# Unsplit float32 projections on quarters of the array, and sums of squares on ScalarE, in a fused attention and gated-MLP kernel

## The chip, the core and the metric

The kernel runs on one core of a Trainium2 chip as one launch. The time is device microseconds (us) of that core, the median of three runs. A core has a matrix engine (TensorE, PE in the profile; PEld is its weight load), a vector engine (VectorE, DVE), an engine for activation functions (ScalarE, ACT), a general one (GpSimd, POOL), and queues that issue DMA transfers (SyncE, SP, issues nearly all of them here). Each engine works through its own instructions in order and waits on semaphores for the others. On-chip data lies in SBUF; matrix products land in PSUM, eight banks of 128 partitions by 512 float32 values.

## The reference, cut to what matters

```python
batch, n_heads, seq, head_dim = 8, 8, 576, 64          # q, k, v; float32
def phi(x):                                            # x scaled by 64 ** -0.25
    proj = x @ omega.T                                 # 64 -> 128 features
    sq = sum(x * x, axis=-1) / 2
    h = proj - sq
    return exp(h - max(h, axis=-1)) / sqrt(128)
q_p, k_p = phi(q_s), phi(k_s)
kv, z = k_p^T @ v, sum(k_p, axis=seq)                  # per batch and head
attn = (q_p @ kv) / (q_p @ z + 1e-6)                   # [4608 tokens, 512]
gate, val = sigmoid(attn @ w_gate), attn @ w_val       # 512 -> 1536
out = (gate * val) @ w_out                             # 1536 -> 512
```

## The kernel before

The program has two stages. The **first stage** holds the attention and, as filler, the early third of the gated products (four of the twelve column tiles of the hidden layer). The **second stage** holds the other eight column tiles (line 558, `gw`) and the output product (line 671, `po`), both with a seven-product scheme for 2 by 2 blocks; the change does not touch their arithmetic, but their banks come from `any_bank`, which it does touch.

**Attention.** Batches are taken in four pairs `u`, heads in four pairs `p`. For one `(u, p)` the two batches have 1152 tokens, nine tiles of 128. A tile of k or q arrives with the 64 dimensions of two heads on the 128 partitions (`raw`, line numbers in `source`). `projected` makes the projection of a group of at most two tiles: ScalarE writes the rounded high part `hi` (L764), GpSimd the rest `lo` (L767), and TensorE does three products of 128 by 128 weights with 256 columns for each tile (L775 to L777), against `omH` and `omL`, which hold omega for both heads in a block-diagonal 128 by 256 matrix, in the type float32r. One bank of PSUM takes two tiles. VectorE takes the row maximum (`mx`, L787), and from it and the sums of squares `sq` the bias terms: `hm` (L793), then for k `nb` (L832), for q `sub` (L898) and the whole exponent `h` (L900). For k, ScalarE does the exponential with a bias for each tile and head, 128 columns at a time (L842), and `pkv` (L867) multiplies with v. For q, TensorE transposes `h` into `pt` (L914), ScalarE takes the exponential into `qp` (L919), `pn` (L931) multiplies with kv, VectorE divides (`den`, `inv`, `x`, L942 to L948), TensorE transposes back into `px` (L956), ScalarE copies it (L965) and SyncE stores it. The float32 products `pkv` and `pn` already use half the columns of the array at a time (64 columns of weights).

**Sums of squares.** `norms` loads q and k a second time with tokens on the partitions (`nat`), a tile of 128 by 512 at a time. ScalarE squares it (L726), VectorE sums each head's 64 columns (L730) and, when the four or five tiles of a batch are there, scales the sums (L747).

**Filler products.** `products` multiplies the finished attention (`xe`, split into two parts by ScalarE at L408 and GpSimd at L418) with the early column tiles: `gv`, L445. Weights that come as float64 words are made into float32 on VectorE and GpSimd (lines 155 to 169, 332) in between. Until the first `xe` is there, each projection is followed by four products into a bank that is never read (`unread`, L781).

**The order.** The order of each engine's work in the first stage is written out by a planner, the class `Turns`: it plays the kernel through with a cost for each instruction (`act`, `dve`, `pool_`, `PE_LAG` and so on) and fixes for each engine which step is next. Steps ask for places (`shelf`): eight banks, of which projections may hold four (`pps`) and filler products two (`gvs`); buffers in SBUF have places of their own. Attention goes by rank, filler products have the lowest rank. The second stage's operands lie in memory that the first stage's buffers held.

Of the kernel before, what the change touches and what calls it, by code (L numbers as in the profile page):

```python
# [9 lines left out]
F32 = mybir.dt.float32  # L10
# [18 lines left out]
GROUPS = {"k": (((0, 1), (2, 3), (4,)), ((5, 6), (7, 8))), "q": (((0, 1), (2, 3)), ((4,), (5, 6), (7, 8)))}  # L29
# [16 lines left out]
UNREAD = 4  # L46

RAWS, SPLITS, KPS, VS, HS, XS, NATS = 6, 5, 8, 3, 4, 3, 2
KVS, PPS, GVS = 13, 4, 2
CVS = 2  # L50
# [122 lines left out]
def attn_glu_kernel(ctx: ExitStack, tc, qT, kT, qn, kn, va, om, ident, w, out):  # L173
# [12 lines left out]
    om_sb = const.tile([P, 2 * M], F32, name="om_sb")  # L186
# [3 lines left out]
    omH = const.tile([P, 2 * M], F32R, name="omH")  # L190
    omL = const.tile([P, 2 * M], F32R, name="omL")
    split(nc, omH, omL, om_sb)
# [3 lines left out]
    def bank(i, name):  # L196
        return ps.tile([P, 512], F32, tag=f"bank{i}", bufs=1, name=name)

    def any_bank(name):

        n_banks[0] += 1
        return bank(n_banks[0] % 8, name)
# [51 lines left out]
    def act(n, pointer=False):  # L254
        return (165 if pointer else 120) + 0.833 * n

    def dve(n):
        return (n + 140) / 0.96

    def dve2(n):  # L260
        return (n / 2 + 140) / 0.96
# [4 lines left out]
    PE_LAG, LAG, ISSUE, LANDS = 260, 100, 420, 3200  # L266


    banks, pps, gvs = shelf(8), shelf(PPS), shelf(GVS)
# [153 lines left out]
    def products():  # L423
        yield from after(x_ready[0][0], 0)
        unread.clear()
        banks.put(spare, turns.now)
# [30 lines left out]
    spare = banks.take()  # L457
    unread = [bank(spare, "unread")]
# [234 lines left out]
    def span(name, b):  # L693
# [5 lines left out]
        "raw": shelf(RAWS), "split": shelf(SPLITS), "kp": shelf(KPS), "v": shelf(VS), "h": shelf(HS), "qp": shelf(HS),  # L699
        "kv": shelf(KVS), "kmid": shelf(NP), "x": shelf(XS), "xs": shelf(2), "nat": shelf(NATS), "x2": shelf(2),  # L700
# [4 lines left out]
    for u in range(U):  # L705
        for b in range(2):
            for n in ("k", "q"):
                sq_ready[n, u, b] = Event(turns)
# [8 lines left out]
    def norms(pool, name, u, b, src):  # L717

        t0, t1 = span(name, b)
        s = pool.tile([P, MID + 1, H], F32, tag="ss", bufs=2, name=f"ss{name}{u}_{b}")[:, : t1 - t0]  # L720
        every = Event(turns, t1 - t0)

        def squares(t, x, i, at):
            at, (k,) = yield from turn("ACT", at, places["x2"])
            x2 = spot(pool, "x2", k, [P, DM], f"x2{name}{u}_{t}")
            nc.scalar.activation(out=x2, in_=x, func=AF.Square)  # L726
            at = use("ACT", at, act(DM), LAG)
            places["nat"].put(i, at)
            at = yield "DVE", at, None
            nc.vector.tensor_reduce(  # L730
                out=s[:, t - t0, :], in_=x2.rearrange("p (h d) -> p h d", d=D), axis=AX.X, op=ALU.add
            )
            at = use("DVE", at, dve(DM), LAG)
            places["x2"].put(k, at)
            every.set(at)

        rank = order["n" + name, u, b]
# [6 lines left out]
        at = yield from after(every, 0)  # L744
        at = yield "DVE", at, None
        sq = pool.tile([P, MID + 1, H], F32, tag="sq", bufs=4 * U, name=f"sq{name}{u}_{b}")
# [3 lines left out]
        at = use("DVE", at, 190, LAG)  # L750
        sqs[name, u, b] = sq
        sq_ready[name, u, b].set(at)

    def projected(pool, name, u, p, b, raw, t0, tiles, at, last):
# [3 lines left out]
        at, (i,) = yield from turn("ACT", at, places["split"])  # L758
        hi, lo = (
            spot(pool, tag, i, [P, 2 * P], f"{tag}{id_}", F32R)[:, : nt * P] for tag in ("hi", "lo")  # L760
        )
        o = (tiles[0] - t0) * P
        x = raw[:, o : o + nt * P]
        nc.scalar.activation(out=hi, in_=x, func=AF.Copy)  # L764
        at = use("ACT", at, act(nt * P), LAG)
        at = yield "POOL", at, None
        nc.gpsimd.tensor_tensor(out=lo, in0=x, in1=hi.bitcast(F32), op=ALU.subtract)  # L767
        at = use("POOL", at, pool_(nt * P), LAG)
        last.set(at)
        at, (place, own) = yield from turn("PE", at, banks, pps)  # L770
        pp = bank(place, f"pp{id_}")[:, : nt * 2 * M]
        for k, t in enumerate(tiles):
            c = slice(k * P, (k + 1) * P)
            o = pp[:, k * 2 * M : (k + 1) * 2 * M]
            nc.tensor.matmul(o, lhsT=lo[:, c], rhs=omH, start=True, stop=False)  # L775
            nc.tensor.matmul(o, lhsT=hi[:, c], rhs=omL, start=False, stop=False)  # L776
            nc.tensor.matmul(o, lhsT=hi[:, c], rhs=omH, start=False, stop=True)  # L777
        at = use("PE", at, 3 * nt * 118, PE_LAG)
        for o in unread:
            for _ in range(UNREAD):  # L780
                nc.tensor.matmul(o[:, : 2 * M], lhsT=hi[:, :P], rhs=omH, start=True, stop=True)  # L781
            use("PE", at - PE_LAG, UNREAD * 118, 0)
        places["split"].put(i, at)
        pp = pp.rearrange("p (i m) -> p i m", m=M)
        at = yield "DVE", at, None
        mx = pool.tile([P, 4], F32, tag="mx", bufs=12, name=f"mx{id_}")[:, : 2 * nt]
        nc.vector.tensor_reduce(out=mx, in_=pp, axis=AX.X, op=ALU.max)  # L787
        at = use("DVE", at, dve(nt * 2 * M), LAG)
        at = yield from after(sq_ready[name, u, b], at)
        at = yield "DVE", at, None  # L790
        s = sqs[name, u, b][:, tiles[0] - t0 : tiles[-1] + 1 - t0, 2 * p : 2 * p + 2]
        hm = pool.tile([P, 2, 2], F32, tag="hm", bufs=12, name=f"hm{id_}")[:, :nt]
        nc.vector.scalar_tensor_tensor(  # L793
            out=hm, in0=mx.rearrange("p (t h) -> p t h", h=2), scalar=SCALE, in1=s,
            op0=ALU.mult, op1=ALU.subtract,
        )
        at = use("DVE", at, 160, LAG)
        return at, id_, pp, hm, s, place, own
# [15 lines left out]
    def keys(pool, u, p, b):  # L814
# [12 lines left out]
        def group(tiles):  # L827
            at_, id_, pp, hm, s, place, own = yield from projected(pool, "k", u, p, b, raw, t0, tiles, at, last)
            nt = len(tiles)
            at_ = yield "DVE", at_, None  # L830
            nb = pool.tile([P, 2, 2], F32, tag="nb", bufs=12, name=f"nb{id_}")[:, :nt]
# [3 lines left out]
            at_ = use("DVE", at_, 160, LAG)  # L835
# [3 lines left out]
            for i, t in enumerate(tiles):  # L839
                kp[t] = x[:, 2 * i : 2 * i + 2, :]  # L840
                for h in range(2):
                    nc.scalar.activation(  # L842
                        out=kp[t][:, h, :], in_=pp[:, 2 * i + h, :], func=AF.Exp,
                        bias=nb[:, i, h : h + 1], scale=SCALE,
                    )
            at_ = use("ACT", at_, 2 * nt * act(M, True), LAG)
# [4 lines left out]
            banks.put(place, at_)  # L851
            pps.put(own, at_)
# [31 lines left out]
    def queries(pool, u, p, b):  # L884
# [6 lines left out]
        def group(tiles):  # L891
            at_ = yield from after(kexp_ready[u, p, b], start)
            at_, id_, pp, hm, s, place, own = yield from projected(pool, "q", u, p, b, raw, t0, tiles, at_, last)
            nt = len(tiles)
            n = 2 * nt
            at_, (hi,) = yield from turn("DVE", at_, places["h"])
            sub = pool.tile([P, 2, 2], F32, tag="sub", bufs=12, name=f"sub{id_}")[:, :nt]
            nc.vector.tensor_tensor(out=sub, in0=s, in1=hm, op=ALU.add)  # L898
            h_sb = spot(pool, "h", hi, [P, 4, M], f"h{id_}")[:, :n]
            nc.vector.scalar_tensor_tensor(  # L900
                out=h_sb,
                in0=pp,
                scalar=SCALE,
                in1=sub.rearrange("p t h -> p (t h)").unsqueeze(2).broadcast_to([P, n, M]),
                op0=ALU.mult,
                op1=ALU.subtract,
            )
            at_ = use("DVE", at_, 240 + dve(n * M), LAG)
            banks.put(place, at_)
            pps.put(own, at_)  # L910
            at_, (place, qi) = yield from turn("PE", at_, banks, places["qp"])
            pt = bank(place, f"pt{id_}")[:, : n * P].rearrange("p (i s) -> p i s", s=P)
            for i in range(n):
                nc.tensor.transpose(out=pt[:, i, :], in_=h_sb[:, i, :], identity=id_sb)  # L914
            at_ = use("PE", at_, n * 109, PE_LAG)
            places["h"].put(hi, at_)
# [34 lines left out]
            at_ = use("DVE", at_, 440 + dve(n * D), LAG)  # L951
# [35 lines left out]
    attended = [U * NP * sum(len(g) for g in GROUPS["q"])]  # L987
# [148 lines left out]
```

## Time and profile before

| | |
|---|---|
| median of 3 runs | 1238.59 us (1237.07 to 1239.68) |
| the profiled execution's own time | 1236.42 us |
| its span, first to last instruction | 1234.6 us |
| mean granted clock of TensorE | 0.966 |
| PE busy | 1138.8 us, 92% |
| DVE busy | 888.4 us, 72% |
| ACT busy | 529.6 us, 43% |
| POOL busy | 572.8 us, 46% |
| second stage's first product (L558) starts at | 581.2 us |

The shares are means over both stages. Busy time of an engine is the time in which at least one of its instructions was in work; matmuls overlap, so the rate of a run of matmuls is read from their starts, not from the mean duration of one. In a row of a group, what stands after the bar is the busy time of the group, the mean duration of one instruction in ns, and the engine's idle time before them with what ended it.

### The profile page before, as it was taken

The page shows a single profiled execution, that of the slowest core. Times are in us where ns is not written, and L with a number is a line of the kernel's source. Part 1 is how long each engine was busy: PE and PEld are TensorE (multiplying, and loading weights), DVE is VectorE, ACT ScalarE, POOL GpSimd, SP SyncE. Part 2 cuts the span into 40 slices and gives each one's busy share as a digit, 9 for nine tenths or more (in the row PEclk, how much of TensorE's full clock was granted, in tenths as well). Part 3 has the DMA queues.
Part 4 walks back from the last instruction along what each step waited for, and adds up shares of the span by engine and source line. Part 5 has one row for each costly group of instructions (what it writes and reads, how often), then busy time and mean ns, then how long its engine had stood idle before and what let it go on. Part 6 is the DMA issues. An engine that isn't in the chain of part 4 may idle for free.

```text
span 1234.6 us, 26447 instructions
## 1 busy us (share of the span) xinstructions
PE 1138.8 (92%) x10092; PEld 1062.0 (86%) x10092; DVE 888.4 (72%) x1885; ACT 529.6 (43%) x1168; POOL 572.8 (46%) x591
## 2 busy tenths in 40 slices
PE   4869989999898998779999999999998899999998
PEld 4758978887787777557999999999998899999998
DVE  5888798898888998623665665666569577777775
ACT  4646676474545554342422323223225243433331
POOL 2647273455635644434566666666657311111111
PEclk7889999999999989888999999999999899999999
DMA  6646477386756755364233233323347675665653
GB/s 234 235 152 220 151 237 242 101 279 234 233 192 217 242 172 171 107 238 140 121 124 123 91 125 124 125 96 124 148 139 252 190 228 184 192 191 188 188 189 112
DMA packets 107744, 217.75 MB, mean 176 GB/s; under 512 B 10848, under 2 KB 48992, under 8 KB 105312
## 3 DMA queue, kind: packets, MB, share of 16 engines
q1 hardware_dynamic: 102288, 206.54, 49.5%
q10 hardware_dynamic: 5328, 9.51, 2.0%
q8 instruction: 80, 1.31, 0.4%
q14 instruction: 48, 0.39, 0.1%
HBM read 141.82 MB, written 74.19 MB: 175 GB/s over the span
## 4 chain that ended last, share of the span: by engine, by line
PE 70%; DVE 11%; issue 6%; POOL 5%; DMA 5%; ACT 2%; SPq 1%; POOLq 0%; DVEq 0%; ACTq 0%
PE gw L558 26%; PE po L671 20%; PE gv L445 8%; PE pnq L931 3%; PE ptq L914 3%; PE pkv L867 2%; DVE mxk L787 1%; PE ppq L775 1%; PE pxq L956 1%; PE ppk L775 1%; DVE hmq L793 1%; DMA ye<-ye 1%; POOL xe L418 1%; PE ppk L777 1%; PE ppk L776 1%
## 5 line engine op out<-in xcount | busy, mean ns | idle before, releaser
L558 PE MATMUL gw<-xl,u 128*128 128x256 f32 x3024 | 363.9, 283 | 6.0 <-DVE u L538 3.8
L558 PEld LDWEIGHTS gw<-xl,u 128*128 128x128 f32 x3024 | 362.2, 190 | 7.6 <-DVE u L538 5.0
L671 PE MATMUL po<-u,yh 128*128 128x256 f32 x1512 | 273.1, 283 | 0.0
L671 PEld LDWEIGHTS po<-u,yh 128*128 128x128 f32 x1512 | 235.1, 191 | 0.0
L671 PE MATMUL po<-u,yl 128*128 128x256 f32 x756 | 214.4, 284 | 5.0 <-POOL yl L147 3.5
L445 PE MATMUL gv<-xe,wh 128*128 128x512 f32 (+1 forms) x640 | 198.0, 386 | 11.4 <-POOL xe L418 11.4
L146 ACT ACTIVATE yh<-yr 128x896 fp32r<-128x896 f32 x108 | 98.9, 948 | 166.8 <-DVE yr L662 58.5
L671 PEld LDWEIGHTS po<-u,yl 128*128 128x128 f32 x756 | 144.7, 191 | 5.6 <-POOL yl L147 3.7
L445 PEld LDWEIGHTS gv<-xe,wh 128*128 128x128 f32 x640 | 116.2, 193 | 32.3 <-POOL xe L418 15.3
L147 POOL TENSOR_TENSOR yl<-yr,yh 128x896 fp32r<-128x896 f32 x18 | 39.3, 2183 | 218.9 <-ACT yh L146 165.9
L445 PE MATMUL gv<-xe,wl 128*128 128x512 f32 (+1 forms) x320 | 123.8, 387 | 12.0 <-ACT xe L408 11.9
L662 DVE TENSOR_TENSOR yr<-yr 128x128 f32<-128x128 f32 x144 | 68.0, 505 | 62.1 <-DMA yr<-ye 61.5
L147 DVE TENSOR_TENSOR yl<-yr,yh 128x896 fp32r<-128x896 f32 x90 | 96.1, 1099 | 12.9 <-ACT yh L146 12.7
L538 DVE TENSOR_TENSOR u<-gw,p 128x256 f32<-128x256 f32 x144 | 60.7, 421 | 60.2 <-PE gw L558 52.1
L767 POOL TENSOR_TENSOR loq<-rawq,hiq 128x256 fp32r<-128x256 f32 (+1 forms) x80 | 60.3, 768 | 83.1 <-ACT hiq L764 57.3
L767 POOL TENSOR_TENSOR lok<-rawk,hik 128x256 fp32r<-128x256 f32 (+1 forms) x80 | 61.5, 777 | 69.4 <-ACT hik L764 64.9
L842 ACT ACTIVATE kpk<-ppk,nbk 128x128 f32<-128x128 f32 x256 | 71.9, 393 | 34.1 <-DVE nbk L832 33.9
L445 PEld LDWEIGHTS gv<-xe,wl 128*128 128x128 f32 x320 | 62.1, 194 | 22.3 <-ACT xe L408 13.1
L591 POOL TENSOR_TENSOR yl<-yl,gl 128x256 f32<-128x256 f32 x36 | 36.0, 1000 | 81.1 <-issue 39.1
L588 ACT ACTIVATE gl<-gl 128x768 f32<-128x768 f32 x36 | 30.5, 846 | 90.0 <-DVE gl L538 90.0
L914 PE MATMUL ptq<-id_sb,hq 128*128 128x128 f32 x288 | 47.4, 284 | 21.9 <-DVE hq L900 19.9
L919 ACT ACTIVATE qpq<-ptq 128x512 f32<-128x512 f32 (+1 forms) x80 | 44.5, 557 | 46.8 <-PE ptq L914 46.1
(218 smaller groups left out, 2209.7 us busy)
## 6 DMA issues: line engine op xcount, KB each, us to landing
yl<-yl SPq DMA_DIRECT2D x36, 896.0 KB, 4.0
yr<-yl SPq DMA_DIRECT2D x72, 448.0 KB, 4.2
xr<-xT SPq DMA_DIRECT2D x68, 256.0 KB, 4.5
u<-w SPq DMA_DIRECT2D x14, 896.0 KB, 6.8
v<-va SPq DMA_DIRECT2D x32, 330.0 KB, 4.4
natk<-kn SPq DMA_DIRECT2D x36, 256.0 KB, 3.5
natq<-qn SPq DMA_DIRECT2D x36, 256.0 KB, 3.2
out<-o ACTq DMA_DIRECT2D x36, 256.0 KB, 2.9
```

Of the source, the lines that this page charges most:

```text
L146: nc.scalar.activation(out=hi, in_=x, func=AF.Copy)
L147: (lo_engine or nc.vector).tensor_tensor(out=lo, in0=x, in1=hi.bitcast(F32), op=ALU.subtract)
L445: nc.tensor.matmul(gv, lhsT=u[:, s], rhs=v, start=(m == 0), stop=(m == 3 * KC - 1))
L538: return nc.vector.tensor_tensor(out=o, in0=a, in1=b, op=ALU.add)
L558: nc.tensor.matmul(o, lhsT=u[:, k, s], rhs=v[:, kc, :], start=(first and m == 0), stop=(m == 5), skip_group_check=not first,)
L662: nc.vector.tensor_tensor(out=raw[:, o], in0=raw[:, a], in1=raw[:, b], op=op)
L671: nc.tensor.matmul(o, lhsT=u[:, i, :], rhs=v[:, k, :], start=(j + m == 0 and n in (1, 6, 5, 4)), stop=(j == NPAIR - 1 and m == 2), skip_gr ...
L767: nc.gpsimd.tensor_tensor(out=lo, in0=x, in1=hi.bitcast(F32), op=ALU.subtract)
L842: nc.scalar.activation(out=kp[t][:, h, :], in_=pp[:, 2 * i + h, :], func=AF.Exp, bias=nb[:, i, h : h + 1], scale=SCALE,)
L914: nc.tensor.transpose(out=pt[:, i, :], in_=h_sb[:, i, :], identity=id_sb)
L919: nc.scalar.activation(out=qp, in_=pt, func=AF.Exp)
L931: nc.tensor.matmul(pn[r, 2 * i + h, :], lhsT=qp[:, 2 * i + h, r], rhs=kvs[u, p, bb][:, h, :], start=True, stop=True,)
```

## The change

Four things are done together.

- **Projection.** The split is gone (`hi`, `lo`, `omH`, `omL`). A tile is projected by four float32 matmuls, one for each quarter of the array: 64 rows (one head's dimensions) by 64 columns (half of the tile's tokens) as weights, and 128 columns of omega moving. The two heads, which use different rows, write to different banks.
- **Groups.** A group has up to four tiles in a place of two banks. There are two such places (`pairs`) and four single banks for all else (`pt`, `pn`, `px`, `pkv`, `gv`). The small steps on VectorE are done once for a group of four. After the projection, q goes on two tiles at a time (`attended_tiles`). `any_bank` of the second stage hands out the four single banks and the four halves of the pairs in turn.
- **Sums of squares.** ScalarE squares each head's 64 columns in place with the scale in the activation and writes the sum by its accumulator: eight instructions for a tile, given out four at a time. VectorE's reduction and scaling are gone.
- **The rest.** The products that nobody reads are gone. The planner's costs and the numbers of buffers are other ones.

```diff
-GROUPS = {"k": (((0, 1), (2, 3), (4,)), ((5, 6), (7, 8))), "q": (((0, 1), (2, 3)), ((4,), (5, 6), (7, 8)))}
+GROUPS = {"k": (((0, 1, 2, 3), (4,)), ((5, 6, 7, 8),)), "q": (((0, 1, 2, 3),), ((4,), (5, 6, 7, 8)))}
-UNREAD = 4
-RAWS, SPLITS, KPS, VS, HS, XS, NATS = 6, 5, 8, 3, 4, 3, 2
-KVS, PPS, GVS = 13, 4, 2
+RAWS, KPS, VS, HS, QPS, XS, NATS = 6, 4, 3, 3, 4, 3, 4
+KVS, GVS, CVS = 15, 2, 2
+BANKS, PAIRS = 4, 2
+    def two_banks(i, name):
+        return ps.tile([P, 2, 512], F32, tag=f"pair{i}", bufs=1, name=name)
     def any_bank(name):
+        i = n_banks[0] % (BANKS + 2 * PAIRS)
         n_banks[0] += 1
-        return bank(n_banks[0] % 8, name)
+        if i < BANKS:
+            return bank(i, name)
+        if not halves:
+            two = two_banks((i - BANKS) // 2, name)
+            halves.extend((two[:, 0], two[:, 1]))
+        return halves.pop(0)
     def act(n, pointer=False):
-        return (165 if pointer else 120) + 0.833 * n
+        return (140 if pointer else 85) + 0.833 * n
     def dve(n):
-        return (n + 140) / 0.96
+        return (n + 65) / 0.96
-    PE_LAG, LAG, ISSUE, LANDS = 260, 100, 420, 3200
+    PE_LAG, LAG, ISSUE, LANDS = 210, 140, 420, 3500
-    banks, pps, gvs = shelf(8), shelf(PPS), shelf(GVS)
+    banks, pairs, gvs = shelf(BANKS), shelf(PAIRS), shelf(GVS)
         def squares(t, x, i, at):
-            nc.scalar.activation(out=x2, in_=x, func=AF.Square)
+            for half in range(2):
+                at = yield "ACT", at, None
+                for h in range(half * H // 2, (half + 1) * H // 2):
+                    part = x[:, h * D : (h + 1) * D]
+                    nc.scalar.activation(
+                        out=part, in_=part, func=AF.Square, scale=SCALE * 0.5**0.5,
+                        accum_out=sq[:, t - t0, h : h + 1],
+                    )
+                at = use("ACT", at, H // 2 * act(D), LAG)
-            nc.vector.tensor_reduce(
-                out=s[:, t - t0, :], in_=x2.rearrange("p (h d) -> p h d", d=D), axis=AX.X, op=ALU.add
-            )
-        nc.vector.tensor_scalar(
-            out=sq[:, : t1 - t0], in0=s, scalar1=SCALE * SCALE / 2.0, scalar2=None, op0=ALU.mult
-        )
     def projected(pool, name, u, p, b, raw, t0, tiles, at, last):
-        nc.scalar.activation(out=hi, in_=x, func=AF.Copy)
-        nc.gpsimd.tensor_tensor(out=lo, in0=x, in1=hi.bitcast(F32), op=ALU.subtract)
-        at, (place, own) = yield from turn("PE", at, banks, pps)
-            nc.tensor.matmul(o, lhsT=lo[:, c], rhs=omH, start=True, stop=False)
-            nc.tensor.matmul(o, lhsT=hi[:, c], rhs=omL, start=False, stop=False)
-            nc.tensor.matmul(o, lhsT=hi[:, c], rhs=omH, start=False, stop=True)
-        at = use("PE", at, 3 * nt * 118, PE_LAG)
-        for o in unread:
-            for _ in range(UNREAD):
-                nc.tensor.matmul(o[:, : 2 * M], lhsT=hi[:, :P], rhs=omH, start=True, stop=True)
+        at, (place,) = yield from turn("PE", at, pairs)
+        pp = two_banks(place, f"pp{id_}").rearrange("p h (t m) -> p h t m", m=M)[:, :, :nt]
+        for k, t in enumerate(tiles):
+            o = (t - t0) * P
+            for one in range(2):
+                for h in range(2):
+                    r = HALVES[one ^ h]
+                    nc.tensor.matmul(
+                        pp[r, h, k, :], lhsT=raw[HALVES[h], o + r.start : o + r.stop], rhs=om_sb[HALVES[h], :],
+                        start=True, stop=True,
+                    )
+        at = use("PE", at, nt * 220 + 100, PE_LAG)
...
+                if i and i % 2 == 0:
+                    at_ = yield "ACT", use("ACT", at_, 4 * act(M, True), 0), None
                 for h in range(2):
                     nc.scalar.activation(
-                        out=kp[t][:, h, :], in_=pp[:, 2 * i + h, :], func=AF.Exp,
+                        out=kp[t][:, h, :], in_=pp[:, h, i, :], func=AF.Exp,
...
+            h_sb = spot(pool, "h", hi, [P, 2, 4, M], f"h{id_}")[:, :, :nt]
+            pairs.put(place, at_)
+            used = Event(turns, (nt + 1) // 2)
+            turns.start(released(used, "h", hi), rank)
+            for i in range(0, nt, 2):
+                turns.start(attended_tiles(h_sb[:, :, i : min(i + 2, nt)], tiles[i : i + 2], at_, used), rank)
+        def attended_tiles(h_sb, tiles, at_, used):
...
-    om = np.zeros((P, 2 * M), omega.dtype)
-    om[:D, :M] = omega.T
-    om[D:, M:] = omega.T
+    om = np.concatenate([omega.T, omega.T], axis=0)
```

More of the change, by code (lines that the diff above doesn't have):

```diff
@@ L423, in products @@
     def products():
-        yield from after(x_ready[0][0], 0)
-        unread.clear()
-        banks.put(spare, turns.now)
         for c, (o, n) in enumerate(chunks):
@@ L707, in attn_glu_kernel @@
             for n in ("k", "q"):
-                sq_ready[n, u, b] = Event(turns)
+                for t in range(*span(n, b)):
+                    sq_ready[n, u, t] = Event(turns)
             for p in range(NP):
@@ L719, in norms @@
         t0, t1 = span(name, b)
-        s = pool.tile([P, MID + 1, H], F32, tag="ss", bufs=2, name=f"ss{name}{u}_{b}")[:, : t1 - t0]
-        every = Event(turns, t1 - t0)
+        sq = pool.tile([P, MID + 1, H], F32, tag="sq", bufs=4 * U, name=f"sq{name}{u}_{b}")
+        sqs[name, u, b] = sq
+        rank = order["n" + name, u, b]
         def squares(t, x, i, at):
[L724 to L727, printed above, removed]
-            places["nat"].put(i, at)
-            at = yield "DVE", at, None
-            nc.vector.tensor_reduce(
-                out=s[:, t - t0, :], in_=x2.rearrange("p (h d) -> p h d", d=D), axis=AX.X, op=ALU.add
-            )
[L733 to L737, printed above, removed]
+            for half in range(2):
[7 more added lines that the diff above has]
+                at = use("ACT", at, H // 2 * act(D), LAG)
+            places["nat"].put(i, at)
+            sq_ready[name, u, t].set(at)
         for t in range(t0, t1):
@@ L757, in projected @@
         nt = len(tiles)
[L758 to L766, printed above, removed]
-        nc.gpsimd.tensor_tensor(out=lo, in0=x, in1=hi.bitcast(F32), op=ALU.subtract)
@@ L787, in projected @@
         nc.vector.tensor_reduce(out=mx, in_=pp, axis=AX.X, op=ALU.max)
         at = use("DVE", at, dve(nt * 2 * M), LAG)
-        at = yield from after(sq_ready[name, u, b], at)
+        for t in tiles:
+            at = yield from after(sq_ready[name, u, t], at)
         at = yield "DVE", at, None
[L791 to L796, printed above, removed]
@@ L797, in projected @@
-        at = use("DVE", at, 160, LAG)
-        return at, id_, pp, hm, s, place, own
+        s = sqs[name, u, b][:, tiles[0] - t0 : tiles[-1] + 1 - t0, 2 * p : 2 * p + 2].rearrange("p t h -> p h t")
+        hm = pool.tile([P, 2, 4], F32, tag="hm", bufs=12, name=f"hm{id_}")[:, :, :nt]
+        nc.vector.scalar_tensor_tensor(out=hm, in0=mx, scalar=SCALE, in1=s, op0=ALU.mult, op1=ALU.subtract)
+        at = use("DVE", at, 100, LAG)
+        return at, id_, pp, hm, s, place
     def source(pool, name, u, p, b, src):
@@ L827, in group @@
         def group(tiles):
-            at_, id_, pp, hm, s, place, own = yield from projected(pool, "k", u, p, b, raw, t0, tiles, at, last)
+            at_, id_, pp, hm, s, place = yield from projected(pool, "k", u, p, b, raw, t0, tiles, at, last)
             nt = len(tiles)
             at_ = yield "DVE", at_, None
-            nb = pool.tile([P, 2, 2], F32, tag="nb", bufs=12, name=f"nb{id_}")[:, :nt]
+            nb = pool.tile([P, 2, 4], F32, tag="nb", bufs=12, name=f"nb{id_}")[:, :, :nt]
             nc.vector.scalar_tensor_tensor(
@@ L834, in group @@
             )
[L835 removed]
+            at_ = use("DVE", at_, 100, LAG)
             tag = "kmid" if tiles[0] == MID else "kp"
@@ L892, in group @@
             at_ = yield from after(kexp_ready[u, p, b], start)
-            at_, id_, pp, hm, s, place, own = yield from projected(pool, "q", u, p, b, raw, t0, tiles, at_, last)
+            at_, id_, pp, hm, s, place = yield from projected(pool, "q", u, p, b, raw, t0, tiles, at_, last)
+            nt = len(tiles)
+            at_, (hi,) = yield from turn("DVE", at_, places["h"])
+            sub = pool.tile([P, 2, 4], F32, tag="sub", bufs=12, name=f"sub{id_}")[:, :, :nt]
+            nc.vector.tensor_tensor(out=sub, in0=s, in1=hm, op=ALU.add)
@@ L894, in group @@
+        def attended_tiles(h_sb, tiles, at_, used):
+            id_ = f"q{u}_{p}_{tiles[0]}"
             nt = len(tiles)
             n = 2 * nt
[L896 to L907, printed above, removed]
@@ L908, in group @@
-            at_ = use("DVE", at_, 240 + dve(n * M), LAG)
-            banks.put(place, at_)
-            pps.put(own, at_)
             at_, (place, qi) = yield from turn("PE", at_, banks, places["qp"])
             pt = bank(place, f"pt{id_}")[:, : n * P].rearrange("p (i s) -> p i s", s=P)
-            for i in range(n):
-                nc.tensor.transpose(out=pt[:, i, :], in_=h_sb[:, i, :], identity=id_sb)
+            for i in range(nt):
+                for h in range(2):
+                    nc.tensor.transpose(out=pt[:, 2 * i + h, :], in_=h_sb[:, h, i, :], identity=id_sb)
@@ L915, in group @@
             at_ = use("PE", at_, n * 109, PE_LAG)
-            places["h"].put(hi, at_)
+            used.set(at_)
             at_ = yield "ACT", at_, None
@@ L986, in attn_glu_kernel @@
                     order[n, u, p, b] = float(len(order))
-    attended = [U * NP * sum(len(g) for g in GROUPS["q"])]
+    attended = [U * NP * sum((len(tiles) + 1) // 2 for g in GROUPS["q"] for tiles in g)]
     keep = ctx.enter_context(tc.tile_pool(name="keep", bufs=1))
```

45 lines of the change are left out of this document (15 added, 30 removed).

## The prediction

> **What bounds the kernel now.** I read the page's busy shares first, then the busy time by stage, because the change touches the first stage only (a row of the windows: the stretch, its length, the busy time of PE, PEld, DVE, ACT and POOL with their instructions, the granted clock, and the DMA's share and GB/s).
>
> ```profile
> span 1234.6 us, 26447 instructions
> PE 1138.8 (92%) x10092; PEld 1062.0 (86%) x10092; DVE 888.4 (72%) x1885; ACT 529.6 (43%) x1168; POOL 572.8 (46%) x591
> ...
> 0.00:124.00 124.00, 87.21 (x960) 79.94 (x962) 97.17 (x213) 68.05 (x190) 64.97 (x68) 0.86 0.62 211
> 124.00:494.00 370.00, 346.37 (x3498) 293.27 (x3495) 325.73 (x772) 211.78 (x587) 187.65 (x200) 0.98 0.61 206
> 494.00:591.00 97.00, 75.26 (x412) 60.76 (x410) 38.39 (x72) 33.09 (x54) 36.25 (x26) 0.88 0.49 173
> 591.00:1234.60 643.60, 629.95 (x5232) 627.99 (x5232) 427.09 (x831) 216.68 (x339) 283.93 (x297) 0.99 0.45 153
> ```
>
> The last window is the second stage: PE is busy 630 of 643.6 us with work that the change leaves alone. What can move is when it starts, and PE's trace has that start, 653 us before the end:
>
> ```profile
> 581.21 7.73 PE L558 MATMUL gw<-xl,u 128*128 128x256 f32 x60
> ```
>
> In the middle window PE is at 346 of 370 us (94%) and DVE at 326 (88%): two engines near full, since the filler products take whatever PE has left. In the early window DVE leads, 97 of 124 us, and PE is idle 37 us. After 494 us attention ends and PE is idle 21.7 us of 97. The chain of waits shows why there:
>
> ```profile
> 482.54 18.11 issue
> 500.69 2.44 POOL c L169
> ...
> 558.10 23.29 PE gv L445 x89
> ```
>
> The late weights (`c`) wait on POOL behind steps of DVE, and the last 89 filler products come at the end of the same chain. So stage one is set by PE's amount of work plus 82 us of PE idle time (37, 24 and 22), 37 of it where DVE is the fuller engine.
>
> **The projections on PE.** The trace of PE, start and duration of each step:
>
> ```profile
> 478.91 0.28 PE L777 MATMUL ppq<-omH,hiq 128*128 128x256 f32 x1
> 479.03 0.28 PE L775 MATMUL ppq<-omH,loq 128*128 128x256 f32 x1
> 479.14 0.28 PE L776 MATMUL ppq<-omL,hiq 128*128 128x256 f32 x1
> 479.26 0.28 PE L777 MATMUL ppq<-omH,hiq 128*128 128x256 f32 x1
> 479.38 0.60 PE L914 MATMUL ptq<-id_sb,hq 128*128 128x128 f32 x4
> 479.91 0.69 PE L931 MATMUL pnq<-kv,qpq 128*64 128x66 f32 x16
> ...
> 479.91 0.55 PEld L931 LDWEIGHTS pnq<-kv,qpq 128*64 128x64 f32 x16 [0.17 <-issue]
> ...
> 481.14 0.69 PE L931 MATMUL pnq<-kv,qpq 128*64 128x66 f32 x16
> 481.76 0.50 PE L445 MATMUL gv<-xe,wl 128*128 128x512 f32 x1
> 482.09 0.63 PE L445 MATMUL gv<-xe,wh 128*128 128x512 f32 x2
> ```
>
> Starts of the split projection lie 0.117 us apart (478.91 to 479.26 in three steps). There are 288 tiles of three, so it takes 864 x 0.117 = 101 us, and at a lower clock early on somewhat more.
>
> The new form is 288 x 4 float32 matmuls. The code has eight matmuls in a full group of `pnq`, the trace 16 records: a float32 matmul is two. So a tile is eight records of 128 columns. Four float32 transposes of 128 columns take 0.53 us (479.38 to 479.91, the change of form included), at most 0.13 for a record; 256 float32r columns took 0.117. I take 0.117 for one record alone, 0.94 us for eight in a row. What overlaps? `pnq` has records of 66 columns on halves of the array's columns. By the same rate a record is 0.06 us and 16 are 0.97; they took 0.62 (481.14 to 481.76): column halves do overlap. No row of this trace shows row halves. From below: all four quarters together, 0.94 / 4 = 0.234 a tile, while eight weight loads at `pnq`'s rate (0.55 / 16) are 0.275. From above: only column halves together, 0.47. I take 0.25, next to the load rate, since the loads are the row that exists: 288 x 0.25 = 72 us. Going in and out of a quartered form costs too. `pnq`'s loads wait 0.17 us for nothing that shows, and the first `gv` after it holds PE for 0.33 us where 0.23 is normal (481.76 to 482.09; 512 columns are two times 0.117). I take 0.2 us for each of the 96 new groups: 19 us, and half of it as the lower end. PE then does 91 us in place of 101, **10 us less**. The ends are 67 + 10 = 77 (24 less) and 135 + 19 = 154 (53 more).
>
> **The products nobody reads.**
>
> ```profile
> L781 PE MATMUL unread<-omH,hik 128*128 128x256 f32 x72 | 13.9, 324 | 0.0
> L781 PE MATMUL unread<-omH,hiq 128*128 128x256 f32 x40 | 6.3, 279 | 0.0
> ```
>
> 112 products, 20 us busy, all in the early window, where PE has 37 us idle. They delay what is behind them in PE's queue (chiefly transposes and `pkv`), but leave no bound; I fold them into the early term. What they may do for the clock: it was 0.86 in that window with PE busy 70% of it, and 0.88 in the window after 494 with 78%. PE would be busy 67 of 124 us.
>
> **What leaves the other engines.**
>
> Groups of VectorE:
>
> ```profile
> L832 DVE SCALAR_TENSOR_TENSOR nbk<-sqk,hmk 128x4 f32<-128x4 f32 (+1 forms) x80 | 30.8, 405 | 0.0
> ...
> L793 DVE SCALAR_TENSOR_TENSOR hmk<-mxk,sqk 128x4 f32<-128x4 f32 (+1 forms) x80 | 24.0, 319 | 0.0
> L730 DVE TENSOR_REDUCE ssq<-x2q 128x8 f32<-128x512 f32 x36 | 23.8, 674 | 1.7 <-ACT x2q L726 1.6
> L730 DVE TENSOR_REDUCE ssk<-x2k 128x8 f32<-128x512 f32 x36 | 23.8, 677 | 8.0 <-ACT x2k L726 8.0
> L793 DVE SCALAR_TENSOR_TENSOR hmq<-mxq,sqq 128x4 f32<-128x4 f32 (+1 forms) x80 | 22.7, 313 | 0.0
> L898 DVE TENSOR_TENSOR subq<-sqq,hmq 128x4 f32<-128x4 f32 (+1 forms) x80 | 21.6, 270 | 0.0
> ```
>
> DVE loses 47.6 us of reductions. The four kinds of small steps go from 80 runs to 48 each: 99 us x 0.4 = 40 less, if a run with eight columns costs what one with four did (they hardly depend on width). The maxima and `h` keep their columns and lose fixed parts, which I leave at zero. That is 88 us of 461 in stage one (97 + 326 + 38). POOL loses the 160 subtractions behind `hi`; it was not full, but two queues leave the way from `raw` to PE.
>
> Groups of ScalarE, and a run of its exponentials from the trace in order of time:
>
> ```profile
> L764 ACT ACTIVATE hik<-rawk 128x256 fp32r<-128x256 f32 (+1 forms) x80 | 30.4, 408 | 23.8 <-PE ppq L777 10.0 <-PE unread L781 6.9 <-DMA rawk<-kT 1.8
> L764 ACT ACTIVATE hiq<-rawq 128x256 fp32r<-128x256 f32 (+1 forms) x80 | 30.3, 414 | 16.5 <-PE ppk L777 6.1 <-PE ppq L777 5.8 <-PE unread L781 2.0
> ...
> L726 ACT ACTIVATE x2q<-natq 128x512 f32<-128x512 f32 x36 | 22.9, 661 | 9.2 <-DMA natq<-qn 6.3 <-DVE ssq L730 2.4 <-ACT x2q L726 0.5
> L726 ACT ACTIVATE x2k<-natk 128x512 f32<-128x512 f32 x36 | 22.7, 634 | 8.6 <-DMA natk<-kn 8.5
> ```
> ```profile
> 469.76 2.18 ACT L842 ACTIVATE kpk<-ppk,nbk 128x128 f32<-128x128 f32 x8 [2.30 <-DVE nbk L832]
> ```
>
> ACT loses 106 us (`hi` and the squares) and gets 576 squares of 64 columns. Eight exponentials of 128 columns with a bias take 2.18 us, about 0.26 each in a row, so 0.15 is the lower end for half as wide ones without a bias. No row shows the accumulator's write; from above I take a second instruction as long as one of these, 0.51 in all. I choose 0.25, nearer to the plain one: 144 us. ACT goes from 313 us in stage one to 351, with ends of 293 and 501.
>
> **The sum.** Of the 288 products at L775, one for each tile, the early window has 67:
>
> ```profile
> 0.00:124.00 124.00, 23.03 (x67) 14.47 (x67) 0.86 0.62 211
> ```
>
> From the profiled execution, 1236.4 us (span 1234.6 and 1.8 around it; the median of the runs is 2.2 above it):
> - PE's projections: -10.
> - Early window: DVE loses about a quarter of its 88 us here (67 of 288 tiles), 22 us of 97. PE waits there for chains that also go through ACT and DMA, so I take half: -11 (0 to -22).
> - Middle window: of PE's 24 us idle half comes back with DVE at some 70%: -12 (0 to -20).
> - After 494: the order will be another one with other planner costs, and the idle 22 us can grow or shrink: 0, plus or minus 10.
>
> Together -33: 1203.4, and **1206 us** as a median of runs. The second stage's PE time is taken as it is: its banks still come round after eight, a pair after both its halves are free.
>
> **The rivals.**
> - *The row halves take turns* (slower). 0.47 us a tile makes the projections 53 us dearer; early and middle idle time takes 11 and 12 of it: 1236.4 + 30 + 2.2 = 1269. It decides from (101 + 23 - 19) / 288 = 0.365 us a tile. For it: the trace has no two row halves at work. Against: `pnq`'s column halves overlap.
> - *ACT becomes the bound.* At 0.51 a square the middle window has 212 + 0.75 x (294 - 106) = 353 of 370 us: fuller than DVE was. Nothing is regained, chains get longer: about 1243. It decides where ACT passes DVE's 326 us, at 0.45 a square.
> - *The quarters overlap in part.* `pnq`'s 0.97 us of records took 0.55 in its loads, 1.76 times on two halves; squared for quarters that is 3.1 of 4, or 0.94 / 3.1 = 0.30 us a tile. The projections then take 87 + 19 us, 5 more than today instead of 10 less: 1221. It is a shade of the row halves' case, and `pnq` is the only row on it. TensorE: Matmul & The Clock Gate in the Trainium skill, Part 3 (Packing small matmuls), gives 3.07 times for four packed tiles of 32 rows, near the same; no run so far shows row tiles here.
> - *The early stage gains nothing, because the array's clock falls.* Without the unread products PE has 67 us of work there at a clock of 0.86. At half speed this is 67 x 0.86 / 0.5 = 115 us of 124, and the -11 is gone: 1217. Against it: 0.86 was granted with 37 us idle. TensorE: Matmul & The Clock Gate in the Trainium skill, Part 1 (The HAM clock gate), says that an idle window of about 3.4 us is enough for half the pulses; the trace's mean neither shows nor excludes such windows.
> - *PSUM places run short.* A group of four k tiles holds a pair for 1.1 us of PE, then some 2 on DVE and 2 on ACT; a q group about 4 in all, so 64 groups and 32 single tiles hold two pairs for some 180 us each out of 490 if nothing queues. If queues double that and PE idles 25 us more in the middle: 1236.4 - 10 - 11 + 25 + 2.2 = 1243. Against: no releaser in the chain is a bank today.
> - *The gain is hidden by the end.* If the chain of late weights after 482 us only moves with the planner's order, the -11 stands and the rest goes: about 1227.
> - *PE fills up.* 0.234 a tile, short changes of form, and nearly all reachable idle time back: -24 - 20 - 20: about 1175.
>
> **How the numbers follow.** Forecast (1188 to 1223) 0.48; quarters in part 0.08; clock 0.05; gain hidden 0.08; PE fills up 0.09; ACT 0.08; places 0.07; row halves 0.07. The first five are faster, less 0.03 at their edges; 0.2% is 2.5 us, about what a measurement of this kernel can tell from no change. Faster 0.75, same 0.05 (those edges and a little of the two at 1243), slower 0.20. A range of 1176 to 1250 leaves out the row halves, the worst of the two at 1243 (0.04 together) and half of "PE fills up".
>
> **What would show it.** Right: `ppk` and `ppq` as 2304 records in the count, about 1.0 to 1.1 us from the first of a full group to the last; DVE in the middle below 75%; ACT there at 60 to 70%; PE idle under 15 us in the middle; `gw` starting near 548 instead of 581 us. Wrong: a group of 1.9 us (row halves in turn); squares spaced by 0.45 us or more; PE waiting at projections for `kpk` or `hq` of two groups before (places); an end still led by late weights with PE idle over 30 us; or a second stage that is no longer 653 us from the first `gw` on.

## The result, and the profile after

The changed kernel takes **1301.75 us** (median of four runs, 1300.0 to 1303.25) against 1238.2 before: 1.0512 times as long, 95% interval 1.0493 to 1.0531. The forecast was 1206, and the range ended at 1250. It is slower by 63.5 us.

The page of the changed kernel and the busy time of its stages, in the columns of the prediction's windows:

```profile
span 1301.0 us, 29349 instructions
PE 1125.4 (86%) x11420; PEld 1014.4 (78%) x11420; DVE 799.6 (61%) x1572; ACT 566.8 (44%) x2087; POOL 452.2 (35%) x431
...
0.00:124.00 124.00, 68.09 (x1098) 57.42 (x1099) 81.28 (x138) 106.53 (x691) 32.37 (x28) 0.85 0.68 228
124.00:494.00 370.00, 340.31 (x4811) 272.22 (x4810) 278.14 (x582) 225.81 (x1030) 117.91 (x94) 0.99 0.65 222
494.00:591.00 97.00, 85.92 (x490) 74.92 (x489) 35.91 (x60) 28.69 (x47) 34.68 (x31) 0.96 0.31 110
591.00:1301.00 710.00, 631.04 (x5028) 609.88 (x5026) 404.23 (x794) 205.82 (x320) 267.30 (x280) 0.99 0.41 136
```

PE, DVE and POOL have less to do, ACT has 37 us more and is far from full over the whole span, and the time is longer: waiting has come in somewhere. The second stage's first product tells the two stages apart. The rows of its tile `gw`, first of the kernel before (first and last start at the end of the row), then of the changed one:

```profile
L558 PE MATMUL gw<-xl,u x3024: 274/282/583, 581.2 to 952.4; 128*128 128x256 f32 x189
```
```profile
L559 PE MATMUL gw<-xl,u x3024: 274/282/582, 545.6 to 1017.5; 128*128 128x256 f32 x189
```

The first stage ends 35.6 us earlier (581.2 to 545.6). But the 3024 products of `gw`, the same on both sides, now take 472 us in place of 371, and from the first of them to the end of the span it is 755.4 us (1301.0 - 545.6) where it was 653.4. The second stage has lost 102 us, the first has won 36, the difference is 66 in the spans.

Where PE waits in it, from the groups of each page, before and after:

```profile
L558 PE MATMUL gw<-xl,u 128*128 128x256 f32 x3024 | 363.9, 283 | 6.0 <-DVE u L538 3.8
```
```profile
L559 PE MATMUL gw<-xl,u 128*128 128x256 f32 x3024 | 392.8, 287 | 75.3 <-DVE gl L539 28.8
```

PE idles 75 us before `gw` where it idled 6, and the group is in work 29 us longer. By an estimate some 17 us of that are tails: a product is 0.28 us long, the next one starts 0.12 us after it when nothing waits, so each of the 105 waits lets 0.16 us more of a last product show. The rest fits some 150 other starts, counted in the trace, that come about 0.1 us late, too little to show as idle time. The trace of the changed kernel in order of time shows one such wait:

```profile
699.72 0.76 PE L559 MATMUL gw<-xl,u 128*128 128x256 f32 x5
...
700.52 0.42 DVE L539 TENSOR_TENSOR gl<-gw,u 128x256 f32<-128x256 f32 x1 [0.29 <-PE gw L559]
...
701.00 4.52 PE L559 MATMUL gw<-xl,u 128*128 128x256 f32 x36 [0.52 <-DVE gl L539]
```

PE ends a product at 700.5, VectorE reads a result out of PSUM until 700.94, and only then does PE's next product begin. In the kernel before the same stretch is one unbroken piece of the chain (`gw`, 325 us for 2718 products). The waits have their own lines in the changed program. In this listing of PE's queue, taken from the two programs, a tile carries its number, and the semaphores that an instruction waits for stand behind it:

```
after   gw0_0_3_4_10076<-xl4_0_9627,u2_7388 128x256 [waits PE_49]
after   gw0_0_3_4_10076<-xl4_4_9755,u2_7388 128x256 [waits Activation_49]
...
before  gw0_0_3_3_10268<-xl3_0_9814,u2_8293 128x256 [waits PE_49]
before  gw1_0_3_3_10269<-xl3_4_9943,u2_8293 128x256 [waits PE_49]
```

These are the first products of two results of one group. Before, the second goes to a tile of its own (10269). After, both results lie in one two-bank tile (10076), in different banks, and the second waits for ScalarE's copy out of the first. That was the theory to test: *a product into one half of a two-bank tile is made to wait for the reader of the other half*. The rival: the second stage suffers from something that the new first stage hands to it (order, operands, memory), or from the number of tiles that come round.

### The profile page after: what moved, and what is told of

Same layout as the page of the kernel before. It is cut to its first block, busy times and chain, and to the rows that moved or that the text cites. A ratio compares the mean times of both kernels' runs of the same rounds, so it can differ in the third digit from the quotient of the medians.

```text
span 1301.0 us, 29349 instructions
## 1 busy us (share of the span) xinstructions
PE 1125.4 (86%) x11420; PEld 1014.4 (78%) x11420; DVE 799.6 (61%) x1572; ACT 566.8 (44%) x2087; POOL 452.2 (35%) x431
## 5 line engine op out<-in xcount | busy, mean ns | idle before, releaser
L559 PE MATMUL gw<-xl,u 128*128 128x256 f32 x3024 | 392.8, 287 | 75.3 <-DVE gl L539 28.8
L559 PEld LDWEIGHTS gw<-xl,u 128*128 128x128 f32 x3024 | 370.5, 191 | 97.2 <-DVE gl L539 35.8
L424 POOL TENSOR_TENSOR xe<-xr,xe 128x512 fp32r<-128x512 f32 (+1 forms) x40 | 49.0, 1242 | 174.5 <-ACT xe L414 168.2
L663 DVE TENSOR_TENSOR yr<-yr 128x128 f32<-128x128 f32 x144 | 65.0, 487 | 56.4 <-DMA yr<-ye 55.9
L765 DVE TENSOR_REDUCE mxk<-ppk 128x8 f32<-128x1024 f32 (+1 forms) x48 | 45.6, 954 | 50.4 <-PE ppk L757 49.8
L731 ACT ACTIVATE natk<-natk 128x64 f32<-128x64 f32 x288 | 69.7, 257 | 9.7 <-DMA natk<-kn 9.6
L731 ACT ACTIVATE natq<-natq 128x64 f32<-128x64 f32 x288 | 69.4, 257 | 3.8 <-DMA natq<-qn 3.8
```

The lines of the kernel that those rows point to most:

```text
L424: nc.gpsimd.tensor_tensor(out=x[:, 1], in0=raw[:, k], in1=x[:, 0].bitcast(F32), op=ALU.subtract)
L559: nc.tensor.matmul(o, lhsT=u[:, k, s], rhs=v[:, kc, :], start=(first and m == 0), stop=(m == 5), skip_group_check=not first,)
L663: nc.vector.tensor_tensor(out=raw[:, o], in0=raw[:, a], in1=raw[:, b], op=op)
L731: nc.scalar.activation(out=part, in_=part, func=AF.Square, scale=SCALE * 0.5**0.5, accum_out=sq[:, t - t0, h : h + 1],)
```

## The experiments

### Eight single banks again in the second stage

```diff
     def any_bank(name):
-        i = n_banks[0] % (BANKS + 2 * PAIRS)
         n_banks[0] += 1
-        if i < BANKS:
-            return bank(i, name)
-        if not halves:
-            two = two_banks((i - BANKS) // 2, name)
-            halves.extend((two[:, 0], two[:, 1]))
-        return halves.pop(0)
+        return second[0].tile([P, 512], F32, tag=f"one{n_banks[0] % 8}", bufs=1, name=name)
...
+    first.close()
+    second.append(ctx.enter_context(tc.tile_pool(name="ps2", bufs=1, space=bass.MemoryType.PSUM)))
```

> The changed kernel, but its second stage takes eight tiles of one bank each from a PSUM pool of its own, as before the change. Theory (shared tiles: a product into one half of a two-bank tile waits for the reader of the other half): the first gw product still starts near 546 us, the time from there to the end falls from 755 to about 653 us, PE's idle time before gw from 75 to under 10 us, and the median to about 1201. Rival (the second stage is slow because its operands or its order changed with the first stage): the 755 us stay and the median is about 1300.

1196.78 us, ratio to before 0.9678 (0.9644 to 0.9712). The rows of `gw` of this run:

```profile
L553 PE MATMUL gw<-xl,u x3024: 274/282/387, 544.1 to 911.5; 128*128 128x256 f32 x189
...
L553 PE MATMUL gw<-xl,u 128*128 128x256 f32 x3024 | 362.0, 282 | 4.9 <-DVE u L533 3.7 <-DVE ye L473 0.8 <-ACT p L564 0.3
```

Idle time before `gw` is down to 4.9 us, and from the first product to the end of the span (1193.2) it is 649 us. The theory's numbers hold, the rival's do not.

### The kernel before with shared tiles in the second stage alone

```diff
     def any_bank(name):
+        i = n_banks[0] % 8
         n_banks[0] += 1
-        return bank(n_banks[0] % 8, name)
+        if i < 4:
+            return second[0].tile([P, 512], F32, tag=f"one{i}", bufs=1, name=name)
+        if not halves:
+            two = second[0].tile([P, 2, 512], F32, tag=f"pair{(i - 4) // 2}", bufs=1, name=name)
+            halves.extend((two[:, 0], two[:, 1]))
+        return halves.pop(0)
...
+    first.close()
+    second.append(ctx.enter_context(tc.tile_pool(name="ps2", bufs=1, space=bass.MemoryType.PSUM)))
```

> The kernel before, whose second stage alone takes its banks as the changed kernel does (four tiles of one bank, four halves of two two-bank tiles). Theory of shared tiles: the first gw product stays near 581 us and the second stage goes from 653 to about 755 us, so about 1340. Rival (the loss comes from the changed first stage): about 1238.

1341.84 us, ratio 1.0848 (1.0817 to 1.088). Its first `gw` starts at 582.8 us, and the rest of the span (1339.4) is 756.6 us:

```profile
L568 PE MATMUL gw<-xl,u 128*128 128x256 f32 x3024 | 395.0, 288 | 75.2 <-DVE gl L548 29.0 <-DVE u L548 16.9 <-ACT p L579 10.3
```

The 75 us of idle time come with the shared tiles and without anything else of the change. The cause is shown from both sides.

### Six tiles, none shared

```diff
-        i = n_banks[0] % (BANKS + 2 * PAIRS)
+        i = n_banks[0] % (BANKS + PAIRS)
...
-        if not halves:
-            two = two_banks((i - BANKS) // 2, name)
-            halves.extend((two[:, 0], two[:, 1]))
-        return halves.pop(0)
+        return ps.tile([P, 512], F32, tag=f"pair{i - BANKS}", bufs=1, name=name)
```

> The changed kernel, but its second stage uses only one bank of each two-bank place, as a tile of one bank: six tiles in turn, none shared. Theory of shared tiles: nearly the time of eight single banks, 1200 to 1215, since three banks a group come round after two groups. Rival (it is the number of tiles that come round, not the sharing): no better than 1300.

1210.16 us, ratio 0.9791 (0.9748 to 0.9834); from the first `gw` (545.1) to the end of the span (1209.6) 664.5 us. Fewer tiles cost some 15 us against the eight of the run above (649), sharing cost 102 against the kernel before. So it is the sharing, and leaving a quarter of PSUM empty would have been much cheaper than sharing it in this way.

### The projections alone: sums of squares back on VectorE

This and the later kernels on the changed one have eight single banks in their second stage, so that the first stage can be judged. This one keeps everything else of the change too: the groups of four, the missing unread products and the planner's costs.

```diff
-                    nc.scalar.activation(
-                        out=part, in_=part, func=AF.Square, scale=SCALE * 0.5**0.5,
-                        accum_out=sq[:, t - t0, h : h + 1],
-                    )
...
+            nc.scalar.activation(out=x2, in_=x, func=AF.Square)
...
+            nc.vector.tensor_reduce(
+                out=s[:, t - t0, :], in_=x2.rearrange("p (h d) -> p h d", d=D), axis=AX.X, op=ALU.add
+            )
```

> The changed kernel with eight single banks in its second stage and with the sums of squares as before the change (one ScalarE square of 512 columns, VectorE sums and scales). It isolates the projections. Theory A (ScalarE paced the first 200 us of the changed kernel, 71 of 76 us busy from 124 to 200): ScalarE falls below 65% there, the first gw product comes 5 to 25 us earlier than 546, about 1185. Theory B (VectorE was the bound, so the moved squares are what brought the 35 us): the first gw product comes later than 546, toward 565, about 1220.

1186.5 us, ratio 0.96 (0.9555 to 0.9645), first `gw` at 532.0. The window from 124 to 200 us, first of the changed kernel, then of this one:

```profile
124.00:200.00 76.00, 62.77 (x972) 52.78 (x974) 57.62 (x119) 71.00 (x468) 23.93 (x21) 0.98 0.85 290
```
```profile
124.00:200.00 76.00, 73.17 (x1175) 61.39 (x1175) 70.08 (x152) 44.83 (x127) 28.71 (x26) 1.00 0.76 259
```

ScalarE falls from 71 to 45 us of 76, PE rises from 63 to 73. Theory A holds: in the changed kernel ScalarE paced this stretch.

### The sums of squares alone, on the kernel before

The edit is the one above the other way round, made to the kernel before.

> The kernel before with only the sums of squares changed: ScalarE squares 64 columns at a time with its accumulator, VectorE's sums and scaling are gone. Theory A (the squares cost ScalarE 0.24 us each, 139 us in all, and it then paces the early stage): ScalarE is busy over 95 of the first 124 us, the first gw product comes later than 581 us, 585 to 600, median 1242 to 1257. Theory B (VectorE is the bound of the first stage, so 55 us less on it come back in part): the first gw product comes at 561 to 571 us, median 1218 to 1228.

1216.93 us, ratio 0.9847 (0.9829 to 0.9865), first `gw` at 563.8: theory B, with the median 1 us below its range. By themselves the moved squares are a gain of 17 us in the first stage, although ScalarE is busy for 99.56 of the first 124 us. So VectorE's work did hold the stage up before. The change without the moved squares brings 49 us (581.2 to 532.0), the moved squares alone 17, and both together 37 (581.2 to 544.1): beside the rest of the change, the squares take back 12 us. Each start is that of one profiled execution; by the medians it is 10 us (1196.78 against 1186.5).

### The planner charged with what a square costs

```diff
-                at = use("ACT", at, H // 2 * act(D), LAG)
+                at = use("ACT", at, H // 2 * 241, LAG)
```

> The changed kernel with eight single banks in its second stage, and the planner charged with the 241 ns that a square with its accumulator takes on the chip, in place of 138. Theory (the plan overbooks ScalarE, so steps queue behind squares that the plan thought done): the first gw product comes 4 to 12 us earlier than 544, median 1185 to 1193. Rival (it is the amount of ScalarE's work, whatever the plan): the first gw product stays at 541 to 547 us, median 1194 to 1200.

1188.2 us, ratio 0.9607 (0.9586 to 0.9629), first `gw` at 536.8. That is 8.6 us less than with 138 ns; the planner's price brings back about 7 of the 12 us. The plan had booked squares on ScalarE at 57% of their cost, and the gain fits the theory that ScalarE's other steps queued behind them.

### The squares shared between the two engines

First by batches: the first batch of each pair on VectorE, the second on ScalarE at 241 ns.

```diff
-                        turns.start(norms(pool, n[1], *a, {"k": kn, "q": qn}[n[1]]), rank)
+                        turns.start((norms, norms_act)[a[1]](pool, n[1], *a, {"k": kn, "q": qn}[n[1]]), rank)
```

> The changed kernel with eight single banks in its second stage; the sums of squares of the first batch of each pair on VectorE as before the change, those of the second batch on ScalarE by its accumulator with the planner charged 241 ns. Theory (two engines near full share the squares best): ScalarE and VectorE both below 85% from 124 to 200 us, the first gw product at 522 to 530 us, median 1175 to 1184. Rival (TensorE's own work bounds the stage once ScalarE is free): as with all sums on VectorE, 530 to 536 us and 1184 to 1190.

1181.71 us, ratio 0.9558 (0.9532 to 0.9585), first `gw` at 529.9: the lowest of all, 55 us below the 1236.34 of the kernel before beside it. The window from 124 to 200 us:

```profile
124.00:200.00 76.00, 72.61 (x1178) 60.26 (x1180) 71.64 (x143) 63.46 (x308) 29.93 (x26) 1.00 0.94 316
```

VectorE is at 94% there, not below 85%, and the start lies at the border of the two expectations (530): against the kernel with all sums on VectorE the ratios' intervals overlap, so what sharing adds to it is not settled.

Then by kind: k on VectorE, q on ScalarE.

> The changed kernel with eight single banks in its second stage; sums of squares of k on VectorE as before the change, those of q on ScalarE by its accumulator with the planner charged 241 ns. Theory (what matters is how the squares are shared, not which): within 5 us of the split by batches, 1177 to 1187. Rival (the first k sums stand at the head of the early stage, and VectorE is slower with them): 1187 to 1195.

1191.31 us, with runs from 1183.71 to 1198.57; ratio 0.9628 (0.9582 to 0.9674), first `gw` at 541.3 in the profiled run. The interval just touches the one of the split by batches. It tends to the rival, but does not decide.

### The products nobody reads

The kernel before with `UNREAD = 0`.

> The kernel before without the 112 products that nobody reads (they are left out, nothing else is). Theory (they fill idle time of TensorE and leave no bound): the median stays within 4 us of 1238. Rival (they keep the clock up): the granted clock of the first 124 us falls from 0.86 to 0.75 or less and the median rises by 5 to 15 us. Rival (they delay the products behind them): 5 to 10 us faster.

1231.55 us, ratio 0.9958 (0.9942 to 0.9973): some 5 us faster, between the first theory and the third. The early window of this run:

```profile
0.00:124.00 124.00, 81.82 (x869) 71.84 (x870) 98.38 (x217) 69.81 (x194) 57.47 (x65) 0.81 0.61 208
```

The granted clock falls from 0.86 to 0.81, far from half, and it costs nothing on balance: the rival of a falling clock is out for the kernel before.

### The planner's costs alone

The kernel before with `act`, `dve`, the costs of small steps, `PE_LAG`, `LAG` and `LANDS` of the changed one.

> The kernel before with only the planner's costs of the changed kernel (activations, VectorE steps, the lags and the landing time of a DMA); no operation is changed. It tells how much of the 35 to 49 us that the first stage gained is the plan alone. Theory (the gain is work taken from VectorE and TensorE): within 6 us of 1236, the first gw product at 575 to 587. Rival (better costs make a tighter plan): 10 to 25 us faster, the first gw product at 556 to 571.

1228.36 us, ratio 0.9922 (0.9905 to 0.9938), first `gw` at 578.5. A better plan is worth 9 us in this comparison, a little over the theory's 6 and short of the rival's 10. The start of `gw` moved by 2.7 us only, but it is that of the slowest of the four runs (1233.68 us).

| kernel | ratio to before (95%) | first `gw`, us | from there to the span's end, us |
|---|---|---|---|
| before | 1 | 581.2 | 653.4 |
| the change | 1.0512 (1.0493 to 1.0531) | 545.6 | 755.4 |
| before, shared tiles in stage two | 1.0848 (1.0817 to 1.0880) | 582.8 | 756.6 |
| the change, eight single banks | 0.9678 (0.9644 to 0.9712) | 544.1 | 649.1 |
| the change, six tiles | 0.9791 (0.9748 to 0.9834) | 545.1 | 664.5 |
| eight single banks, sums on VectorE | 0.9600 (0.9555 to 0.9645) | 532.0 | 649.3 |
| eight single banks, squares at 241 ns | 0.9607 (0.9586 to 0.9629) | 536.8 | 649.7 |
| eight single banks, squares shared by batches | 0.9558 (0.9532 to 0.9585) | 529.9 | 652.3 |

## Why the prediction was wrong

**The step that failed** is the last sentence of the sum: "The second stage's PE time is taken as it is: its banks still come round after eight, a pair after both its halves are free." It looked only at when a place is handed out again, and there it found no wait. It did not look at what holds between two users of one place while both are at work. The results of a group are written and read in turn: product 1 into the first bank, ScalarE's copy of it while product 6 runs into the second, and so on. That overlap rests on the banks being separate objects for whoever sets the semaphores. With two results in one tile, write and read alternate. The price is 102 us over 72 groups, 1.4 us a group, and no term, rival or bound of the prediction contained it. The list of signs at its end did name "a second stage that is no longer 653 us from the first `gw` on", but gave it no mechanism. The places rival looked for PSUM trouble in the first stage, at the two pairs; it was in the second, at the same pairs.

**The first stage came out as forecast, 35.6 us earlier against 33, but not by the forecast's terms.**

- *Projections.* The group of four, in PE's trace of the changed kernel:

```profile
255.33 1.10 PE L757 MATMUL ppq<-om_sb,rawq 64*64 64x128 f32 x32
256.37 0.69 PE L912 MATMUL pnq<-kv,qpq 128*64 128x66 f32 x16
```

  32 records in 1.04 us, 0.26 us a tile; 0.25 was taken. Eight records one after the other were put at 0.94 us; by that estimate the quarters overlap 3.6 times. The rivals in which row halves take turns (1.9 us a group) or overlap in part (1.2) are out.
- *Squares.* The trace of ScalarE:

```profile
6.26 0.24 ACT L731 ACTIVATE natk<-natk 128x64 f32<-128x64 f32 x1
6.40 0.18 ACT L731 ACTIVATION_READ_ACCUMULATOR natk<-natk 128x1 f32 x1
6.49 0.24 ACT L731 ACTIVATE natk<-natk 128x64 f32<-128x64 f32 x1
```

  The accumulator is read by a second instruction, and a square with it takes 0.24 us from start to start; 0.25 was taken.
- *PE's work and its idle time.* The whole of stage one as one window, before and after:

```profile
0.00:581.20 581.20, 501.18 (x4800) 426.73 (x4801) 458.04 (x1049) 308.80 (x823) 288.86 (x294) 0.94 0.59 199
```
```profile
0.00:545.60 545.60, 459.15 (x6129) 371.02 (x6130) 372.28 (x736) 345.50 (x1742) 169.72 (x134) 0.96 0.62 212
```

  PE is busy 42 us less and idle 6 us more (86.4 for 80.0). The forecast had 10 us less work and 23 us of idle time regained: each term wrong, their sum right by chance. Counted in the traces from each product's start to the next one's start, or to its own end if that comes first, the projections went from 122 to 86 us, where 101 to 91 was taken: the 101 is the pace inside a full run of them, 0.117 us. The unread products, 17 us by this count, were put into the idle term, and the transposes took 12 us more. Of the idle time, the early window was to give back 11 us and lost 19 (56 for 37), the middle window was to give back 12 and lost 6 (29.7 for 23.6). ScalarE took VectorE's place: 106.5 of the first 124 us, where VectorE had 97. With the squares back on VectorE, PE's idle time from 124 to 200 us falls from 13.2 to 2.8 us, so there ScalarE is the cause. In the first 124 us it falls only from 56 to 50, still above the 37 of the kernel before: that part is open. The unread products no longer count as work there, and the clock is lower (below). The rival "ACT becomes the bound" had been put off to a square of 0.45 us by the mean of the middle window. It decides earlier, at 0.24, because the planner lets the squares run ahead, and they fill ScalarE in the first 200 us (106.5 + 71.0 busy, with over 900 of the squares' 1152 instructions) instead of being spread evenly.
- *VectorE* is busy 86 us less (458.0 to 372.3); 88 were taken.
- *The end of stage one*, left at 0 plus or minus 10, lost its idle time: from 494 us to the first `gw`, PE is busy 50.55 of 51.4 us,

```profile
494.00:545.40 51.40, 50.55 (x223) 41.22 (x222) 12.85 (x17) 13.16 (x22) 19.45 (x14) 1.00 0.30 104
```

  where the kernel before had idled 19.6 us from 494 to its first `gw` (80.0 less 36.8 and 23.6). That hid what the early and middle windows lost. The sign "PE idle under 15 us in the middle" had failed, while the record count, the length of a group and the start of `gw` came out.

**Two rules weighed.** *Packing.* The rival "the quarters overlap in part" stood on 0.30 us a tile, and 0.26 were measured. TensorE: Matmul & The Clock Gate in the Trainium skill, Part 3 (Packing small matmuls), gives 3.07 times for four packed tiles of 32 rows. That is another packing than the 64 by 64 quarters here, and no run has it.

*The clock.* The rows grant the changed kernel 0.85 in the early window, and 1.00 in the first 31 us of it. The pace of the projections there says otherwise:

```profile
15.01 1.99 PE L757 MATMUL ppk<-om_sb,rawk 64*64 64x128 f32 x32 [3.79 <-ACT kpk L820]
...
76.42 1.99 PE L757 MATMUL ppk<-om_sb,rawk 64*64 64x128 f32 x32
```

A full group takes 1.99 us at 15.0 us, as it does at 76.4, where the row's clock is 0.50 (64.8 to 78.3 us); at 255.3 it takes 1.10. (So this is not the sign of row halves in turn, which was put at 1.9.) The trace has no record of the clock before 44.2 us, and a row counts the time before as full speed. In the kernel before the records start at 11.1 us, and the starts of the split projections are 0.21 us apart before that and 0.12 behind it. So the array worked at half pace until 44 us in the changed kernel, and until 11 us in the kernel before; the condition of the rival "the array's clock falls" was met in good part. By Part 1 (The HAM clock gate) of TensorE: Matmul & The Clock Gate in the Trainium skill the clock could have fallen to half in the early stage. The 1.99 us for 1.10 agree with that. What it cost is open: PE has 56 us of idle time in that window, ScalarE is the fuller engine there, and no run changes the clock alone. The run without unread products, made on the kernel before, has its first record at 12.5 us and shows no loss.

## What to carry to other kernels

When a change merges buffers into one object, look at every user of the old ones, also in stages that the change doesn't mean: ask which write ran beside which read, and whether whoever places the waits can still tell the two apart. The reuse distance of a place says nothing about that. And a sum that fits is no proof of its terms: read busy and idle time of the bounding engine apart, and look at the stretch where moved work really lands, not at the mean.

## What was not expected of the hardware

- Four float32 matmuls on 64 by 64 quarters run nearly side by side: 32 records, each of 128 columns, in 1.04 us, 33 ns a record. The column halves of `pnq`, with 66 columns a record, need 39 ns (16 in 0.62 us). Shared out over four quarters and two halves, that is 32 columns in 33 ns and 33 columns in 39: the quarters keep about the pace of the halves.
- A sum by ScalarE's accumulator costs a second instruction; the square starts the next one 0.14 us later, the read of the accumulator 0.10.
- A row's granted clock is no measurement before the trace's first record of the clock. The changed kernel's rows say 1.00 for the first 31 us, while groups of projections run at half their later pace until 44 us. The spacing of equal products is the check.
